# Nineteen of the 36 v tiles are issued from the POOL queue instead of SP

## The chip, the cores and the metric

One core of a Trainium2 chip runs the kernel. The metric is the device time of one launch in microseconds (us): the median of the runs. Work is spread over TensorE (PE in the profile), VectorE (DVE), ScalarE (ACT), GpSimd (POOL) and SyncE (SP), which only issues DMAs here. Each engine runs its own list of instructions in order, and they wait for each other through semaphores.

## The reference, cut to what matters

Attention within chunks of 64 rows, for 8 batches, 8 heads, 576 rows and 64 columns a head; then a channel mix on the rows of all heads (x, 4608 x 512).

```python
scores = scale * np.matmul(q_c, k_c.transpose(0, 1, 2, 4, 3))      # chunks of 64
attn = np.exp(scores - max); attn = attn / (sum(attn) + 1e-09)
out = np.matmul(attn, v_c)
# x = out with the heads side by side; x_prev = x one row earlier
xk = mu_k * x + (1.0 - mu_k) * x_prev
xr = mu_r * x + (1.0 - mu_r) * x_prev
k = np.maximum(xk @ w_k, 0.0)
v = k * k @ w_v
r = 1.0 / (1.0 + np.exp(-(xr @ w_r)))
return (r * v).astype(np.float32)
```

## The kernel before

The 4608 rows are cut into 36 tiles of 128 rows (t, two chunks each) and 18 groups of 256 rows (g, two tiles each). From group 4 on, two groups make a pair (p = 2 to 8), whose products with w_k and w_v are made by seven half-size products instead of eight, with sums of weights that are made once, stored to a DRAM tensor `kept` and fetched again for each pair from p = 3 on.

Nothing is scheduled by a planner: the work is cut into some 2,000 steps, and the string ORDER (lines 23 to 196) writes out the order by hand. A word such as `P12.1:A` is step 1 of task P12 on engine A (ScalarE; D is VectorE, G is GpSimd). The loop at the end of the function takes the words one by one, so each engine and each DMA queue gets its instructions in the order of the string. For a load, the letter is the queue: none or D means SP, A means ScalarE, G means GpSimd's queue, POOL (`queue`). Tiles lie at fixed columns of two SBUF arenas (`plain` and `rounded`; the table PLACE), and one stretch of columns serves many tiles in turn. An instruction that writes a stretch waits until the earlier reader of it is done; here a stretch that a tile waits for is called its slot.

The steps that the change and the prediction touch:

- `v{t}.0` (load_v, L491): loads the v tile of tile t, four DMAs of 64 KB, each 64 partitions x 4 heads x 64 elements of four bytes.
- `bq{g}`, `bk{g}` (load_blocks, L519 and L521): q and k of a group, in four steps each of 4 to 8 DMAs, from SP. VectorE turns them in blocks of 32 (att_qk, L689, `D{t}`).
- `S{t}` (L714): scores. `Z{g}`: softmax of a group on VectorE and ScalarE (L778 is its maximum, which waits for the scores of both tiles). `P{t}.0` (L831) transposes the weights, `P{t}.1` moves them, and `P{t}.2` (L844) multiplies them with the v tile into x; this is the only reader of v{t}.
- `K`, `R`, `V` of the first four groups (L1084, L1130, L1163), with `V{g}{tl}.8` (L1175) on VectorE, and for the pairs `M` (L1398), `C` (L1412), `F` (L1442), `V{n}_{p}` (L1488).
- `Y{n}{u}.2` (L1282) and `kr` (L1299): stores of weight sums to `kept`, from SP. `Xt4_3.1` (L1366) writes where the sum of Y41 lay, so it waits for that store.
- `L{n}{u}_{p}` and `Lr{i}_{p}` (L1305): fetches from `kept`, four or eight DMAs of 128 KB, from POOL. `Q{c}{tl}_{p}` (L1150): stores of the output of a pair, from POOL.

In ORDER v4 to v12 stand ahead of the first fetch and the first store of POOL. v17 stands between Q10_2 and L61_3, v20 between L61_4 and L40_4, v21 between Q00_3 and L60_4, v23 between L71_4 and L41_4, v24 between L61_5 and L50_5, v26 between L40_5 and L70_5, v30 between Q11_5 and Q01_5, v29 between L50_6 and Lr1_7, v32 between Q10_6 and L50_7, v35 between L51_7 and Lr0_8.

```python
def queue(e):
    return {"A": nc.scalar, "G": nc.gpsimd}.get(e, nc.sync)
...
        def fn(on):
            vt = new(f"v{t}", [HP, 2, D])
            ...
                    queue(on).dma_start(
```

Of the kernel before, what the change touches and what calls it, by code (L numbers as in the profile page):

```python
# [57 lines left out]
K30.0 V21.6 V21.7 bq6.1 bq7.3 kr.1 bq7.1 Ar4.0:D Z5.0:D Z5.1:D bq6.2 bq6.0 bq6.3 bk6.1 bk6.3 bk6.0
Z5.2:A Ar4.1:A Ak4.2:A Ak4.0:D D14.0:D D15.0:D Hr13.0:D Hr03.0:D Hr13.1:D Hr03.1:D A4.0:A Ak4.1:A
Z5.3:D Z5.4:D K31.3:D V20.8:D Y0.0:D Br4.0:D D13.0:D Bk4.1:D K30.1:A K30.2:A K30.3:A K30.4:D K32.0  # L60
P10.0 V31.0 P11.0 V21.8:D Hk14.0:D V30.0 V30.1 V31.1 K32.1:A K32.2:A U71.0:A Hr04.0:D V21.9 V20.9
bk7.3 bk7.0 U70.0:D P11.1:A U70.1:D K31.4:D K33.1:A V30.2 V30.3 V31.2 K33.2:A K33.3:A P10.1:D
K32.3:D U71.1:D K32.4:D D12.0:D Ar4.2:A K33.4:D V30.4 v11.0 v10.0 D13.1:D D12.1:D Br4.1:D Bk4.0:D
# [6 lines left out]
Hr15.0:A Hr15.1:D C21.0:A C21.1:D Y1.2:D Y71.0:A bk8.1 bk8.0 bk8.2 bq8.1 Ec11_20.1:A Xt4_2.0:A Y50.2  # L70
bq8.0 bk8.3 Y1.4:D D15.1:D D14.1:D Y70.2 V31.9 bq8.3 Y60.1:D Xt3_2.1:D Y1.5:D D16.1:D M20.4 C20.2:A
F1_20.0:A F1_20.1:D M20.5 P12.0 P13.0 M21.5 C20.3:A Ec11_21.0:A Y51.0:A M21.4 C21.2:A M20.6 V30.9
kr.0 Y51.1:D Y71.1:D Y60.2 v13.0 v12.0 Y61.0:D Ec11_21.1:A C21.3:A C20.5:D Ec22_20.0:A Hr05.0:A
P12.1:A Xt4_2.1:D D17.1:D M21.2 C21.4:D Ak9.0:D Hr05.1:D M20.2 P13.1:A Ec22_20.1:A C20.4:D Y61.1:D
M21.6 Ec21_21.0:A C21.5:D F4_20.0:A F4_20.1:D F1_21.0:D Ec21_21.1:A Ec22_21.0:A Ec21_20.0:A S14.0
# [11 lines left out]
D20.1:D Br7.0:D Bk7.0:D Z8.0:D X_3.0:D X_3.1:D X_3.2:D R61.0 M30.1 C30.0:A Hr07.0:A R60.1:A
Xt1_3.0:A Xt2_3.0:A Xb22_3.0:A R61.1:A M31.0 Xt1_3.1:D C30.1:D M31.1 Xt3_3.0:A C31.0:A Z8.1:D
X_3.3:D Xt2_3.1:D Q01_2.0 Y40.2 Q11_2.0 Q10_2.0 v17.0 L61_3.0 M30.4 bq10.0 bq9.0 bq9.3 bk9.2 Y51.2
L51_3.0 bk9.3 bk9.1 bk9.0 Y41.2 bq9.1 bq10.3 bq10.1 C31.1:D M30.5 M31.5 M31.4 A7.0:A Z8.2:A  # L90
Ec11_30.0:A Xt3_3.1:D Xb22_3.1:D Ec11_30.1:A C30.2:A D21.1:D Ec11_31.0:A C31.3:A Z8.3:D Z8.4:D M31.6
Xt4_3.0:D F1_30.0:A F1_30.1:D Xt4_3.1:D C30.3:A C31.2:A Hr17.0:A M30.6 C31.5:D Hr17.1:D C30.5:D
# [6 lines left out]
V5_3.0 F6_31.0:A F7_30.0:A R70.1:A O3.0:A v19.0 L71_3.0 L60_3.0 L70_3.0 Lr0_4.0 L40_3.0 L41_3.0
F_30.2:D F6_30.0:D F2_30.1:D Br8.0:D F6_30.1:D Br8.1:D P18.0 P19.0 V5_3.1 bq11.0 bq10.2 bq11.2  # L100
Ak8.1:A F2_31.0:A F6_31.1:D Ak8.0:D F7_31.1:D Bk8.0:D V2_3.0 Hr08.0:A Hk08.0:A V6_3.0 V6_3.1 O3.2:A
F2_31.1:D F7_30.1:D Hr18.0:D P18.1:D O3.1:A Ak8.2:A F_30.3:D D20.0:D V2_3.1 D21.0:D F_31.3:D P19.1:D
F3_31.0:A V7_3.0 V7_3.1 O3.3:D Hr08.1:D F3_30.0:D Hk08.1:D O3.6:D O3.4:D P18.2 P19.2 S20.0 S21.0
F3_31.1:D Z10.0:D Ar9.2:A Br9.1:D F3_30.1:D O3.8:D Lr1_4.0 M40.0 V4_3.0 V4_3.1 V3_3.0 Z10.1:D V3_3.1
Hr18.1:D Ak9.1:A Bk9.0:D Bk8.1:D R81.0 bq11.3 bq11.1 bk11.0 bk11.2 bk11.3 bk11.1 bq12.1 bq12.0
C40.0:A Ak9.2:A O3.5:D O3.9:D Hk18.0:A A9.0:A Ar9.1:A R81.1:A Bk9.1:D R80.0 R80.1:A Xb22_4.0:A
Hk18.1:D X_4.0:D O3.7:D X_4.1:D D22.0:D Xt1_4.0:D Xt1_4.1:D X_4.2:D M40.1 M41.0 Xt2_4.0:A Xt2_4.1:D
C40.1:D Br9.0:D M40.4 Ec11_40.0:D Xb22_4.1:D X_4.3:D M41.4 Xt3_4.0:D Hr09.0:D Z10.2:A C40.2:A
C41.0:A Ec11_40.1:A M40.5 M40.2 M41.5 C40.3:A C41.2:A M41.2 Xt3_4.1:D Z10.3:D Z10.4:D P20.0 M40.6
Xt4_4.0:A Hr19.0:A P21.0 Hr09.1:D D23.0:D C40.4:D bk12.2 bq12.3 L61_4.0 v20.0 C41.3:A M41.6 D23.1:D  # L110
Ec21_40.0:A Ec21_40.1:A C40.5:D D22.1:D Ec22_40.0:A Ec22_40.1:A P21.1:A F1_40.0:A C41.4:D P20.1:D
C41.5:D M41.1 C41.1:D Xt4_4.1:D L40_4.0 v22.0 bk13.3 Q10_3.0 L50_4.0 Q11_3.0 L70_4.0 Q01_3.0 Q00_3.0
v21.0 bq12.2 bq13.2 bk12.0 bk12.1 bk12.3 bq13.1 L60_4.0 L51_4.0 L71_4.0 v23.0 bq13.3 bk13.1 bk13.0
bk13.2 bq13.0 F1_40.1:D Ec22_41.0:A Ec22_41.1:A P20.2 S22.0 S23.0 P21.2 F4_40.0:A Z11.0:D F4_40.1:D
F4_41.0:A Ec11_41.0:A Ak10.1:A A10.0:A V1_4.0 M40.3 Ec21_41.0:A F_40.0:D Ec11_41.1:A F5_40.0:A
# [1503 lines left out]
```

## Time and profile before

| | us |
|---|---|
| median of 3 runs | 651.52 |
| lowest and highest | 649.33 and 654.31 |
| the profiled execution | 645.9 |
| its span, first to last instruction | 644.1 |
| busy in the span: TensorE, VectorE, ScalarE, POOL | 576.5, 530.0, 406.9, 181.2 |

The profile is of one execution. Busy time is that of an engine's own instructions; the issue of DMAs on SP isn't counted as busy, and "SPq" is SP's queue. A row of the timeline has the start, the length, the engine and line, the operation, its tiles as written <- read, and in brackets the idle time ahead of it with what ended it. A wait is put down to what came last.

### The profile page before, as it was taken

The numbers are of one execution on the slowest core, as the hardware profiler recorded it, in microseconds if no ns is written. First come the engines' busy times: TensorE is split into PE (matmuls) and PEld (weight loads), VectorE is DVE, ScalarE is ACT, GpSimd is POOL, SyncE is SP. The second block draws the span as 40 slices with busy tenths as digits, with TensorE's granted clock in tenths as the row PEclk, the third lists the DMA queues.
The fourth block names the chain that finished last, engine by engine and source line by source line (L and its number), as shares of the span: only waits on it lengthen the run. The fifth ranks groups of instructions, "written<-read, shape, count | busy, mean of one in ns | idle before, by whom it ended". The sixth has DMA issues, their size and how long they took to land.

```text
span 644.1 us, 16103 instructions
## 1 busy us (share of the span) xinstructions
PE 576.5 (90%) x6183; PEld 533.7 (83%) x6183; DVE 530.0 (82%) x889; ACT 406.9 (63%) x804; POOL 181.2 (28%) x338
## 2 busy tenths in 40 slices
...
GB/s 203 256 211 254 84 69 42 95 92 111 75 73 69 207 123 190 112 191 162 204 206 259 82 205 47 245 77 90 216 159 222 155 127 196 100 194 37 156 140 66
DMA packets 229438, 93.38 MB, mean 145 GB/s; under 512 B 181481, under 2 KB 221425, under 8 KB 229361
## 3 DMA queue, kind: packets, MB, share of 16 engines
...
## 4 chain that ended last, share of the span: by engine, by line
PE 53%; SPq 19%; DVE 12%; DMA 8%; issue 4%; ACT 4%; POOLq 0%; DVEq 0%; ACTq 0%; POOL 0%
PE o L1488 17%; PE m L1398 14%; SPq L521 14%; PE pr L1130 10%; SPq L491 4%; PE pv L1163 3%; DMA plain<-in_k 2%; PE xps L844 2%; PE s L714 2%; DMA plain<-in_v 2%; DMA plain<-in_q 1%; PE pt L831 1%; DVE plain L689 1%; ACT rounded L412 1%; DMA plain<-in_moe_w_v 1%
## 5 line engine op out<-in xcount | busy, mean ns | idle before, releaser
L1305 POOL DMA_DIRECT2D rounded<-kept x288 | 155.1, 555 | 372.4 <-PE pr L1130 256.6
L1398 PE MATMUL m<-rounded 128*128 128x256 f32 x1176 | 148.8, 286 | 12.4 <-DVE plain L1412 12.4
L1398 PEld LDWEIGHTS m<-rounded 128*128 128x128 f32 x1176 | 145.7, 194 | 14.1 <-DVE plain L1412 12.8
L1488 PE MATMUL o<-rounded 128*128 128x256 f32 x1176 | 151.2, 288 | 4.3 <-DVE rounded L1442 4.3
L1488 PEld LDWEIGHTS o<-rounded 128*128 128x128 f32 x1176 | 146.8, 195 | 6.0 <-DVE rounded L1442 4.7
L412 ACT ACTIVATE rounded<-plain 128x512 fp32r<-128x512 f32 (+1 forms) x151 | 97.3, 662 | 62.8 <-PE o L1488 13.6
L1130 PE MATMUL pr<-rounded 128*128 128x512 f32 x432 | 103.8, 394 | 0.1
L1130 PEld LDWEIGHTS pr<-rounded 128*128 128x128 f32 x432 | 80.2, 190 | 16.7 <-DVE plain L1506 0.5
L1007 ACT ACTIVATE plain<-xps,mu 128x256 f32<-128x256 f32 x128 | 54.3, 486 | 37.0 <-PE xps L844 21.7
L1442 DVE TENSOR_TENSOR rounded<-plain,rounded 128x512 fp32r<-128x512 f32 x98 | 65.6, 682 | 4.7 <-ACT rounded L412 2.0
L1013 ACT ACTIVATE plain<-xps,mu 128x255 f32<-128x255 f32 (+3 forms) x176 | 62.3, 448 | 0.0
L1084 PE MATMUL pk<-rounded 128*128 128x256 f32 x384 | 50.1, 290 | 9.8 <-DVE plain L1175 6.2
L1084 PEld LDWEIGHTS pk<-rounded 128*128 128x128 f32 x384 | 48.5, 197 | 12.2 <-issue 6.6
L689 DVE STREAM_TRANSPOSE plain<-plain 128x512 f32<-128x512 f32 x60 | 41.2, 698 | 19.1 <-DMA plain<-in_q 12.4
L844 PE MATMUL xps<-plain 64*64 64x64 f32 x1152 | 30.5, 241 | 24.9 <-DMA plain<-in_v 24.3
L844 PEld LDWEIGHTS xps<-plain 64*64 64x64 f32 x1152 | 25.3, 152 | 29.4 <-DMA plain<-in_v 19.5
L1163 PE MATMUL pv<-rounded 128*128 128x512 f32 x192 | 49.4, 409 | 0.0
L1024 DVE TENSOR_TENSOR plain<-plain 128x512 f32<-128x512 f32 x64 | 43.1, 680 | 2.0 <-ACT plain L1013 1.9
L1163 PEld LDWEIGHTS pv<-rounded 128*128 128x128 f32 x192 | 36.6, 197 | 7.5
L1073 ACT ACTIVATE plain<-plain 128x512 f32<-128x512 f32 x61 | 37.4, 628 | 5.0 <-DVE plain L1065 4.5
L778 DVE TENSOR_REDUCE mg<-s 128x16 f32<-128x1024 f32 x15 | 18.3, 1220 | 26.6 <-PE s L714 26.5
L1450 DVE TENSOR_TENSOR plain<-plain 128x512 f32<-128x512 f32 x56 | 38.0, 685 | 0.6
...
## 6 DMA issues: line engine op xcount, KB each, us to landing
rounded<-kept POOLq DMA_DIRECT2D x288, 128.0 KB, 3.6
plain<-in_v SPq DMA_DIRECT2D x144, 64.0 KB, 2.9
...
plain<-in_q SPq DMA_DIRECT2D x160, 32.0 KB, 2.3
plain<-in_k SPq DMA_DIRECT2D x160, 32.0 KB, 2.4
...
```

The lines of the kernel that those rows point to most:

```text
L412: nc.scalar.activation(to, x, AF.Copy)
L521: queue(e).dma_start(out=to_s[:, i], in_=of[:, i])
L844: nc.tensor.matmul(T[f"xps{g}"][halves[c], 2 * j + a, tl * TT + e * CH : tl * TT + (e + 1) * CH], T[f"v{t}"][halves[j], hp, e, :], T[f"pT{ ...
L1007: nc.scalar.activation(now(nm, h)[:, c], xps()[:, cb], AF.Copy, scale=mu2[:, 0, i, cb : cb + 1])
L1013: nc.scalar.activation(before(nm)[:, cb, s : s + n], xps()[:, cb, s - 1 : s - 1 + n], AF.Copy, scale=mu2[:, 1, i, cb : cb + 1],)
L1084: nc.tensor.matmul(pk[:, e, :], wk_at(f // 4)[:, a, cb, f % 4 * P : (f % 4 + 1) * P], x[:, b, cb, :], start=(n == 0), stop=(n == 3 * NB - 1),)
L1130: nc.tensor.matmul(pr, xr_at(g, a, cb)[:, tl * TT : (tl + 1) * TT], wr_of(g, cb // 2)[:, b, cb % 2, :], start=(n == 0), stop=(n == 3 * NB ...
L1163: nc.tensor.matmul(pv, kk_at(g, a, f // 2)[:, f % 2, tl * TT : (tl + 1) * TT], wv_at(f // 4)[:, :, b, f % 4, :], start=(f == 0 and n == 0) ...
L1305: nc.gpsimd.dma_start(out=to[:, c : c + 256], in_=of[:, c : c + 256])
L1398: nc.tensor.matmul(ps[w][:, e, :], left(n, a, cb, 2 * u + e), right(g, n, b, cb), start=first and i == 0, stop=i == 11, skip_group_check=True,
L1442: engine[e].tensor_tensor(form(p, n, u, 1), r(i), f32(form(p, n, u, 0)), ALU.subtract)
L1488: nc.tensor.matmul(ps[w][:, tl, :], form(p, n, u, a)[:, e, tl * TT : (tl + 1) * TT], moving(n, b, 2 * u + e), start=first and i == 0, stop ...
```

## The change

Nineteen words of ORDER get the ending `:G`, so the four DMAs of each of these tiles are issued on POOL's queue instead of SP's: v4, v5, v6, v7, v9, v8, v11, v10, v12, v17, v20, v21, v23, v24, v26, v30, v29, v32 and v35, in this order. Their place among the words stays, and so does everything else. The other seventeen (v0 to v3, v13 to v16, v18, v19, v22, v25, v27, v28, v31, v33, v34) stay on SP. The lines of the string are wrapped anew, which makes up most of the diff; three of its places:

```diff
-V01.1 V10.0 P4.0 V00.1 P5.0 K11.1:A cwv1.3:D hwv1.0:D hwv1.1:D K11.2:A P4.1:A V01.2 V00.2 v4.0 v5.0
-D6.0:D D7.0:D cwv2.3:D K13.3:A P5.1:A hwv2.0:A D7.1:D V00.3 S6.0 P4.2 S7.0 P5.2 V11.0 K13.4:D
+V01.1 V10.0 P4.0 V00.1 P5.0 K11.1:A cwv1.3:D hwv1.0:D hwv1.1:D K11.2:A P4.1:A V01.2 V00.2 v4.0:G
+v5.0:G D6.0:D D7.0:D cwv2.3:D K13.3:A P5.1:A hwv2.0:A D7.1:D V00.3 S6.0 P4.2 S7.0 P5.2 V11.0 K13.4:D
...
-Q10_5.0 Q11_5.0 bk17.3 bq17.3 Xt1_6.1:D Br13.0:D Xt2_6.1:D O5.7:D v30.0 R120.0 Q01_5.0 L60_6.0
+Q10_5.0 Q11_5.0 bk17.3 bq17.3 Xt1_6.1:D Br13.0:D Xt2_6.1:D O5.7:D v30.0:G R120.0 Q01_5.0 L60_6.0
...
-Hr116.0:A O7.3:D v34.0 v35.0 V3_7.1 O7.5:D Br16.0:D Hk016.1:D Hr016.0:D P34.2 P35.2 Hr116.1:D
+Hr116.0:A O7.3:D v34.0 v35.0:G V3_7.1 O7.5:D Br16.0:D Hk016.1:D Hr016.0:D P34.2 P35.2 Hr116.1:D
```

## Rows read from the trace of the kernel before

**Rows 1.** The page: busy time of TensorE; chain that ended last, by engine
```profile
PE 576.5 (90%) x6183; PEld 533.7 (83%) x6183; DVE 530.0 (82%) x889; ACT 406.9 (63%) x804; POOL 181.2 (28%) x338
...
PE 53%; SPq 19%; DVE 12%; DMA 8%; issue 4%; ACT 4%; POOLq 0%; DVEq 0%; ACTq 0%; POOL 0%
```

**Rows 2.** Waits: who waited for what, us in total, times, longest
```profile
DVE mg L778 <- PE s L714: 26.5, 5, 10.7
PE xps L844 <- DMA plain<-in_v: 24.3, 10, 8.2
...
DVE rounded L1366 <- DMA kept<-rounded: 13.6, 1, 13.6
...
DVE plain L689 <- DMA plain<-in_q: 12.4, 5, 6.6
...
DVE plain L689 <- DMA plain<-in_k: 6.6, 5, 3.6
```

**Rows 3.** Timeline of TensorE: the first matmuls behind its longest stops
```profile
87.81 0.47 PE L844 MATMUL xps<-plain 64*64 64x64 f32 x2 [4.34 <-DMA plain<-in_v]
...
163.99 1.41 PE L1084 MATMUL pk<-rounded 128*128 128x256 f32 x5 [6.23 <-DVE plain L1175]
...
183.63 1.02 PE L844 MATMUL xps<-plain 64*64 64x64 f32 x8 [8.00 <-DMA plain<-in_v]
...
292.28 6.66 PE L1398 MATMUL m<-rounded 128*128 128x256 f32 x36 [12.05 <-DVE plain L1412]
...
394.03 2.29 PE L1488 MATMUL o<-rounded 128*128 128x256 f32 x9 [3.62 <-DVE rounded L1442]
...
435.17 0.47 PE L844 MATMUL xps<-plain 64*64 64x64 f32 x2 [8.19 <-DMA plain<-in_v]
...
497.23 0.32 PE L844 MATMUL xps<-plain 64*64 64x64 f32 x2 [2.17 <-DMA plain<-in_v]
```

**Rows 4.** Busy time by stretch, PEclk the granted clock; one of seven, their sum
```profile
184.00:191.00 7.00, 6.59 (x132) 5.64 (x132) 1.78 (x3) 3.74 (x11) 0.00 (x0) 0.50 0.38 67
...
sum 37.00, PE 34.52 PEld 31.00 DVE 20.02 ACT 11.72 POOL 0.00; mean PE 4.93 PEld 4.43 DVE 2.86 ACT 1.67 POOL 0.00
```

**Rows 5.** Lines L491 and L1305: issues in ns (min/median/max); L1305's landing
```profile
L491 SPq DMA_DIRECT2D plain<-in_v x144: 595/614/1415, 3.6 to 547.3; - x144
...
L1305 POOL DMA_DIRECT2D rounded<-kept x288: 527/541/767, 237.1 to 619.0; - x144
...
DMA to landing us min/median/max: 2.5/3.6/5.8
```

**Rows 6.** Timeline of the SP queue: issues of v tiles, and of stores to kept
```profile
85.54 11.31 SPq L491 DMA_DIRECT2D plain<-in_v  x16
...
178.49 5.21 SPq L491 DMA_DIRECT2D plain<-in_v  x8
...
252.25 0.34 SPq L1282 DMA_DIRECT2D kept<-rounded  x1
266.91 2.58 SPq L491 DMA_DIRECT2D plain<-in_v  x4
...
284.86 0.45 SPq L1282 DMA_DIRECT2D kept<-rounded  x1
```

**Rows 7.** Timeline of VectorE: last readers of the slots of v4, v10, bq10; Xt4_3.1
```profile
65.76 1.22 DVE L603 TENSOR_TENSOR rounded<-plain,rounded 128x1024 fp32r<-128x1024 f32 x1
...
158.73 1.28 DVE L1045 TENSOR_TENSOR rounded<-plain,rounded 128x512 fp32r<-128x512 f32 x2
...
253.72 0.69 DVE L1442 TENSOR_TENSOR rounded<-plain,rounded 128x512 fp32r<-128x512 f32 x1 [0.29 <-PE o L1488]
...
289.73 0.69 DVE L1366 TENSOR_TENSOR rounded<-plain,rounded 128x512 fp32r<-128x512 f32 x1 [13.56 <-DMA kept<-rounded]
```

**Rows 8.** Timeline of POOL: its first DMAs, and the fetches around v24's place
```profile
237.15 6.15 POOL L1305 DMA_DIRECT2D rounded<-kept  x11 [219.37 <-PE pr L1130]
...
410.24 1.60 POOL L1305 DMA_DIRECT2D rounded<-kept  x3 [0.67 <-issue]
```

More of the change, by code (lines that the diff above doesn't have):

```diff
@@ L58 @@
[L58 to L63, printed above, removed]
@@ L70 @@
[L70 to L75, printed above, removed]
@@ L87 @@
[L87 to L92, printed above, removed]
@@ L99 @@
[L99 to L104, printed above, removed]
@@ L105 @@
[L105 to L115, printed above, removed]
-Ec21_41.1:A Ec12_40.0:A Hr19.1:D Z11.1:D F_40.1:D Ak10.0:D Bk10.0:D F_40.2:D D24.0:D Ar10.0:D
@@ L129 @@
-Q11_4.0 L51_5.0 Q10_4.0 L61_5.0 v24.0 L50_5.0 M51.4 M50.1 Xb22_5.0:A C50.1:D Z12.2:A Z12.3:D M51.5
-C51.3:A Ar11.2:A Xb22_5.1:D Ec11_50.0:D Z12.4:D Br11.1:D M50.4 C50.2:A M50.5 C50.3:A C51.2:A M51.6
-Xt4_5.0:A C51.5:D Xt4_5.1:D Ec11_50.1:D P24.0 P25.0 M50.6 M51.2 M50.2 C50.5:D F1_50.0:D D29.0:D
-C51.4:D M51.1 Ec21_51.0:D Hr011.0:A C50.4:D Hr011.1:D Ec22_50.0:A Ec22_50.1:A F4_50.0:A F4_50.1:D
-F1_50.1:D Ak12.0:D Hr111.0:A Ec22_51.0:A Ec21_51.1:A Ec22_51.1:A F4_51.0:A Ec21_50.0:D Ec21_50.1:A
-P24.1:A C51.1:D M50.3 M51.3 V1_5.0 Ec11_51.0:D F4_51.1:D Ec11_51.1:A P25.1:A S26.0 P24.2 P25.2 S27.0
+Ar2.1:A A2.0:A v6.0:G v7.0:G Ak2.2:A Br2.0:D Ak2.0:D Bk2.1:D D8.1:D Bk2.0:D Hk02.0:D Ar2.2:A
@@ new lines @@
+Hr02.0:A V01.8:D Hk02.1:D V00.8:D Br2.1:D Hk12.0:D Hk12.1:D K22.0 U1.1:D U0.4:D bq4.1 bq4.2 bq4.3
+bq4.0 U1.4:D D8.0:D V10.8:D Hr12.0:A U50.0:D P7.1:A P6.1:A S8.0 P6.2 P7.2 Ak3.0:D U50.1:D D9.0:D
+V11.8:D Hr02.1:D Hr12.1:D S9.0 U0.2:D U0.3:D bq5.2 V01.9 bq5.0 bk5.2 bq5.3 bq5.1 V11.9 bk5.0 V00.9
+bk5.3 V10.9 bk6.2 Ak3.2:A Bk3.1:D U1.6:D U0.5:D U1.3:D U1.5:D Hk13.0:A Hk13.1:D Z4.0:D K20.0 K20.1:A
+K21.0 R21.0 R20.0 U51.0:A Ak3.1:A K20.2:A Z4.1:D Bk3.0:D U0.6:D U1.7:D Z4.2:A K21.1:A Hk03.0:D
+K20.3:D Hk03.1:D D11.0:D U60.0:D K22.1:A U31.0:A Ar3.2:A Z4.3:D U60.1:D A3.0:A R20.1:A U61.0:A
@@ new lines @@
+K20.4:D U0.7:D Ar3.0:D Z4.4:D K22.2:A K21.2:A K21.3:A K21.4:D U51.1:D K31.0 U30.0:D R21.1:A Br3.1:D
+D10.0:D U30.1:D U61.1:D K22.3:A K23.0 V21.0 V21.1 V20.0 V20.1 V20.2 P8.0 K31.1:A K22.4:D K23.1:A
+K31.2:A Ar3.1:A Br3.0:D U31.1:D P9.0 P9.1:A K23.2:A v9.0:G v8.0:G P8.1:D bq7.2 bk5.1 bq7.0 D11.1:D
+D10.1:D V21.2 V20.3 V20.4 K23.3:A K23.4:D Ar9.0:D V20.5 V21.3 P8.2 P9.2 S10.0 S11.0 V21.4 V20.6
+K33.0 V20.7 V21.5 K30.0 V21.6 V21.7 bq6.1 bq7.3 kr.1 bq7.1 Ar4.0:D Z5.0:D Z5.1:D bq6.2 bq6.0 bq6.3
+bk6.1 bk6.3 bk6.0 Z5.2:A Ar4.1:A Ak4.2:A Ak4.0:D D14.0:D D15.0:D Hr13.0:D Hr03.0:D Hr13.1:D Hr03.1:D
@@ new lines @@
+A4.0:A Ak4.1:A Z5.3:D Z5.4:D K31.3:D V20.8:D Y0.0:D Br4.0:D D13.0:D Bk4.1:D K30.1:A K30.2:A K30.3:A
+K30.4:D K32.0 P10.0 V31.0 P11.0 V21.8:D Hk14.0:D V30.0 V30.1 V31.1 K32.1:A K32.2:A U71.0:A Hr04.0:D
+V21.9 V20.9 bk7.3 bk7.0 U70.0:D P11.1:A U70.1:D K31.4:D K33.1:A V30.2 V30.3 V31.2 K33.2:A K33.3:A
+P10.1:D K32.3:D U71.1:D K32.4:D D12.0:D Ar4.2:A K33.4:D V30.4 v11.0:G v10.0:G D13.1:D D12.1:D
+Br4.1:D Bk4.0:D V30.5 P10.2 P11.2 S12.0 S13.0 Hk14.1:D Hk04.0:D Hk04.1:D Z6.0:D Ak5.0:D V31.3
+Hr04.1:D Ak5.1:A Y0.3:D Y1.1:D Hr14.0:D V31.4 V31.5 R31.0 V30.6 V31.6 V30.7 V31.7 R30.0 Ar5.1:A
@@ new lines @@
+Ak5.2:A Bk5.0:D Y0.1:D Y0.2:D R31.1:A Y70.0:A Y0.4:D Y50.0:A Ar5.0:D Hr14.1:D Z6.1:D Y0.5:D Bk5.1:D
+Z6.2:A V31.8:D X_2.0:D X_2.1:D Y70.1:D Xb22_2.0:A Xb22_2.1:D Z6.3:D R40.0 M20.0 Xt3_2.0:A R30.1:A
+Y50.1:D Br5.0:D X_2.2:D Z6.4:D R40.1:A Ar5.2:A A5.0:A C20.0:A M20.1 C20.1:D Ec11_20.0:A Y60.0:A
+V30.8:D Y1.3:D Br5.1:D Y1.0:D R41.0 Xt2_2.0:A Xt1_2.0:A R41.1:A X_2.3:D M21.0 M21.1 Xt1_2.1:D bk7.1
+bk7.2 Xt2_2.1:D Hr15.0:A Hr15.1:D C21.0:A C21.1:D Y1.2:D Y71.0:A bk8.1 bk8.0 bk8.2 bq8.1 Ec11_20.1:A
@@ new lines @@
+Xt4_2.0:A Y50.2 bq8.0 bk8.3 Y1.4:D D15.1:D D14.1:D Y70.2 V31.9 bq8.3 Y60.1:D Xt3_2.1:D Y1.5:D
+D16.1:D M20.4 C20.2:A F1_20.0:A F1_20.1:D M20.5 P12.0 P13.0 M21.5 C20.3:A Ec11_21.0:A Y51.0:A M21.4
+C21.2:A M20.6 V30.9 kr.0 Y51.1:D Y71.1:D Y60.2 v13.0 v12.0:G Y61.0:D Ec11_21.1:A C21.3:A C20.5:D
+Ec22_20.0:A Hr05.0:A P12.1:A Xt4_2.1:D D17.1:D M21.2 C21.4:D Ak9.0:D Hr05.1:D M20.2 P13.1:A
+Ec22_20.1:A C20.4:D Y61.1:D M21.6 Ec21_21.0:A C21.5:D F4_20.0:A F4_20.1:D F1_21.0:D Ec21_21.1:A
+Ec22_21.0:A Ec21_20.0:A S14.0 P12.2 S15.0 P13.2 F1_21.1:D Y1.6:D Y1.7:D Ec21_20.1:A Z7.0:D
@@ new lines @@
+Ec22_21.1:A F4_21.0:D Ak6.0:D F_20.0:D A6.0:A Ak6.1:A Bk6.0:D Z7.1:D F_20.1:D F_20.2:D Ar6.1:A
+Ar6.0:D V1_2.0 M21.3 M20.3 F4_21.1:D Ec12_20.0:A F_21.0:D F5_20.0:A F5_20.1:D F_21.1:D V1_2.1 R50.0
+Z7.2:A F6_20.0:A R51.0 F_21.2:D Z7.3:D bk10.3 v14.0 Y71.2 bq8.2 bk10.2 bk10.1 R50.1:A Ec12_20.1:A
+O2.0:A V5_2.0 F2_20.0:A F6_21.0:D F6_20.1:D Z7.4:D Ec12_21.0:A R51.1:A V6_2.0 F5_21.0:A Ec12_21.1:A
+F7_20.0:A F6_21.1:D D17.0:D F2_20.1:D D16.0:D P14.0 V6_2.1 F7_20.1:D Br6.0:D F2_21.0:A Hk06.0:A
+O2.2:A F7_21.0:A P15.0 F2_21.1:D V2_2.0 F_20.3:D F7_21.1:D V7_2.0 F3_20.0:D F_21.3:D Hk06.1:D
@@ new lines @@
+F5_21.1:D P14.1:A Ak6.2:A Ar6.2:A P15.1:A V2_2.1 F3_20.1:D Y0.6:D Bk6.1:D V7_2.1 Y41.0:D Y0.7:D
+V5_2.1 Y40.0:A O2.3:D Y40.1:D Br6.1:D bk10.0 Y61.2 v15.0 bq9.2 S16.0 S17.0 P14.2 P15.2 O2.1:A V3_2.0
+Y41.1:D F3_21.0:A Hr16.0:A F3_21.1:D Ar7.0:D O2.4:D O2.6:D Ak7.2:A Lr0_3.0 Lr1_3.0 M30.0 V3_2.1
+Hr06.0:A Ar7.2:A Ak7.1:A Hk16.0:A Ak7.0:D O2.8:D Bk7.1:D O2.5:D Hr06.1:D V4_2.0 Ar7.1:A Hr16.1:D
+V4_2.1 R60.0 O2.7:D Br7.1:D Hk16.1:D O2.9:D D20.1:D Br7.0:D Bk7.0:D Z8.0:D X_3.0:D X_3.1:D X_3.2:D
+R61.0 M30.1 C30.0:A Hr07.0:A R60.1:A Xt1_3.0:A Xt2_3.0:A Xb22_3.0:A R61.1:A M31.0 Xt1_3.1:D C30.1:D
@@ new lines @@
+M31.1 Xt3_3.0:A C31.0:A Z8.1:D X_3.3:D Xt2_3.1:D Q01_2.0 Y40.2 Q11_2.0 Q10_2.0 v17.0:G L61_3.0 M30.4
+bq10.0 bq9.0 bq9.3 bk9.2 Y51.2 L51_3.0 bk9.3 bk9.1 bk9.0 Y41.2 bq9.1 bq10.3 bq10.1 C31.1:D M30.5
+M31.5 M31.4 A7.0:A Z8.2:A Ec11_30.0:A Xt3_3.1:D Xb22_3.1:D Ec11_30.1:A C30.2:A D21.1:D Ec11_31.0:A
+C31.3:A Z8.3:D Z8.4:D M31.6 Xt4_3.0:D F1_30.0:A F1_30.1:D Xt4_3.1:D C30.3:A C31.2:A Hr17.0:A M30.6
+C31.5:D Hr17.1:D C30.5:D Ec22_31.0:A Ec11_31.1:D Ec22_31.1:A Ec22_30.0:A Ec22_30.1:A D19.1:D M31.2
@@ new lines @@
+C31.4:D D18.1:D F1_31.0:A F1_31.1:D D18.0:D v16.0 P16.0 P17.0 M30.3 M31.3 D19.0:D F4_31.0:A
+F4_31.1:D Ec21_31.0:D P17.1:A P16.1:A M30.2 S18.0 Ec21_31.1:A Ec12_31.0:A F4_30.0:D Hr07.1:D S19.0
+C30.4:D Z9.0:D P16.2 P17.2 Ec21_30.0:A F_31.0:D F5_31.0:A Ec21_30.1:A F4_30.1:D Z9.1:D Z9.2:A
+F_30.0:D F_31.1:D F_31.2:D F5_30.0:D F_30.1:D F5_30.1:D R71.0 R70.0 V1_3.0 L50_3.0 v18.0 Ec12_30.0:A
+Ar8.2:A Ec12_30.1:A F2_30.0:A Z9.3:D Ar8.0:D F5_31.1:D Z9.4:D Ec12_31.1:A R71.1:A Q00_2.0 Ar8.1:A
+F7_31.0:A V1_3.1 V5_3.0 F6_31.0:A F7_30.0:A R70.1:A O3.0:A v19.0 L71_3.0 L60_3.0 L70_3.0 Lr0_4.0
```

92 lines of the change are left out of this document (41 added, 51 removed).

## The prediction

> **What bounds the kernel now.** I read the page's first part and the chain first. TensorE is busy 576.5 us of 644.1, so 68 us at most are idle on the engine that carries the work. The chain that ended last gives TensorE 53%, but 19% to the issue on the SP queue and 8% to DMAs [rows 1]: a queue that only hands out loads holds about 122 us of it. The reader should ask next whether TensorE really stands still for those loads. The waits say yes: it waited 24.3 us for v tiles, in ten pieces [rows 2]. VectorE waited 12.4 and 6.6 us for q and k loads, 13.6 us for the landing of a store to `kept`, and 26.5 us for scores that come behind a late tile; together 59.1 us [rows 2].
>
> The timeline of TensorE then gives each stop a place. I number the seven that matter by what ended them [rows 3]: (a) 4.34 us before 87.81, v4; (b) 6.23 before 163.99, VectorE at L1175; (c) 8.00 before 183.63, v10; (d) 12.05 before 292.28, VectorE at L1412; (e) 3.62 before 394.03, VectorE at L1442; (f) 8.19 before 435.17, v24; (g) 2.17 before 497.23, v28. Their sum is 44.60 us. Each stop also costs clock: in seven stretches behind them, 37 us together, the granted clock is at or near 0.50, the lower of its two levels, as in the one shown, and TensorE is busy 34.52 us there [rows 4]; the same work at the higher level needs about half, so up to 17.3 us lie there.
>
> **Why the loads are late.** SP takes 614 ns to issue one v DMA [rows 5], four to a tile, 2.6 us with the gaps (four tiles in 11.31 us [rows 6]). Nineteen tiles are 19 x 2.6 = 49 us of a queue that issues one instruction after the other. Tile v10 is handed out from 181 to 184, in the second half of the eight issues from 178.49 [rows 6], while its slot had been free since the subtraction that ends by 160.0 [rows 7]; v4 goes out at 85.54 although the last reader of its slot ended at 67.0 [rows 6, 7]. So these tiles are late because of SP's place in its list, not because of memory.
>
> **The change part by part.** Nothing is removed; 76 DMAs go to another queue.
>
> *SP loses 49 us of issue.* (a), (c) and (f) are waits for tiles that move. v4 to v12 are nine tiles, and POOL is empty where they stand: it idles 219.37 us before its first DMA at 237.15, so since 17.8 [rows 8]. So v4 and v10 go out when their slots come free, at 67.0 and 160.0, 18 and 21 us before they did. v24 stands on POOL behind the fetch that ends near 411, 16 us ahead of the stop at 427.0 [rows 8, 3]; its slot holds k10, read last by the scores of tiles 20 and 21, far earlier. (g) waits for v28, which stays on SP but stands behind v30 and v29 in the order; both leave, two tiles are 5.2 us [rows 6], and the stop is 2.17. These four: 22.70 us.
>
> (b) comes from a VectorE wait of up to 6.6 us for a q load [rows 2]. Six tiles have left SP ahead of it: four of 11.31 us and two more of about 5.2, 16.5 us [rows 6]. (a) takes 4.3 of that lead, because TensorE and VectorE come earlier too, so 12 us stay against 6.6 and the 2 us of the k wait before it. The cover is thin, and a slot that comes free late could use it up.
>
> (d) is the largest. SP stops after the store at 252.25 and starts again with v17 at 266.91: 14.3 us in which the whole queue stood behind v17's slot [rows 6]. Eight blocks later it issues the store of a `kept` block at 284.86 [rows 6], and VectorE's wait of 13.56 us ends at 289.73, just behind that landing [rows 7]; L1412 follows, and TensorE goes on at 292.28. With v17 on POOL, SP goes on once bq10's slot is free, at 254.4 [rows 7]; the work from the end of v17 at 269.5 to that store was 15.3 us, so it is issued at 269.7 and, with the same 4.8 us to land, is there at 274.5. VectorE came to it at 276.2. (d) goes, by 1.7 us. Behind v17 on POOL wait the fetches of pair 3, which it holds until about 271 (266.9 and 4.4); they are in rival 2.
>
> (e) comes from VectorE, which waits for k and q loads just before: the longest of its k waits, 3.6 us [rows 2]. v20, v21 and v23 leave SP ahead of them: 3 x 2.6 = 7.8 us. It goes.
>
> *POOL gains 76 issues.* No v DMA was on POOL, so the price is bounded: a fetch there takes 541 ns for 128 rows of 1 KB [rows 5], and a v DMA has 256 rows of 256 B. Flat, it is 0.55 us; if it goes with the rows, 1.1. I take the upper end, as the rows are what differ: 4.4 us a tile. For the first nine tiles that hides in POOL's idle time [rows 8]. The other ten put 22 to 44 us more between the weight fetches; these are issued ahead of their use, and what it costs if that cover is gone is rival 2. A v DMA lands about as late as a fetch, 3.6 us [rows 5], against the 16 us that v24 has.
>
> *A rule that speaks against the change.* The 288 fetches were issued in 527 to 767 ns each, over 380 us of the run, and landed in 5.8 us at the latest [rows 5]. The Trainium skill, "SBUF — State Buffer", section "SBUF: two separate sides", says that DMAs from the POOL queue have their descriptors written by GpSimd, which VectorE locks out during some copies. By that rule an issue beside such a copy would be stretched, by the row it is stretched to 767 ns at most, 3.1 us a tile; the sum is the same by the row, and the rule's case is the third rival below.
>
> **The sum.** 44.60 us idle in full. Of the 17.3 us at the lower clock I take half, 8.6: not each stop will close wholly, and VectorE's own waits, 59.1 us, cap what both engines can gain. Total 53 us. Against the execution's own time, 645.9 us (span 644.1 and 1.8 around it), that is 593. The median of the runs shown is 651.5, 5.6 above that execution; I carry the 53 over: 598.5, and call it 599.
>
> **The rivals.**
>
> 1. *Only the direct waits go.* SP's freed time is eaten: it stops in order at the next slot that is not free, as it does at v17, and q, k and the store come no earlier. Then (a), (c), (f), (g) remain, 22.70 of 44.60 us, with their share of the clock 27: 624.5 us. For it: SP already stands still at one place [rows 6], so issue is not its only limit. Against it: at (d) the tile on which it stands is one of those that leave.
>
> 2. *The fetches pay.* Ten of the tiles stand among the weight fetches on POOL, 2.2 to 4.4 us each. If all of that delayed weights that TensorE waits for, 22 to 44 us come back: 620 to 642, say 631. Against it: none of its seven stops is for a fetch, the largest waits of TensorE are for v tiles and VectorE [rows 2, 3].
>
> 3. *Slower: POOL is held at each issue.* The eight tiles v4 to v10 go out one behind the other from 67.0, 32 DMAs. At X us each v10 is there at 67.0 + 32 X; TensorE wants it at 175.6 and got it at 183.6. With each DMA held as long as the slowest landing, 5.8 us, that is 252.6, 69 us later than now, and what (d) to (g) still give, about 31, does not pay for it: 690. It decides from X = (183.6 - 67.0 + 31) / 32 = 4.6 us on. The Trainium skill's rule of the section above would be its cause. Against it: 767 ns is the longest of 288 [rows 5].
>
> 4. *No change.* The tiles would still be late, say because they wait for their slots and not for SP. Against it: 18 and 21 us between free slot and issue. 651.5.
>
> **How the numbers follow.** The forecast has 0.70; rival 1 0.17, rival 2 0.07, rival 3 0.03, rival 4 0.03. The prediction is the likeliest, 599. Low end: all 44.6 and all 17.3 us, and some 4.6 from smaller stops not counted: 585. High end: rival 1, 624. That leaves out rivals 2 in part, 3 and 4, and ends below 585: under 2 in 10. About 1% is what a measurement of this kernel can tell from no change (its three runs spread by 0.8%). Faster by over 1%: 0.70 + 0.17 + 0.07 = 0.94; same 0.03; slower 0.03.
>
> **What would show it.** Right: TensorE's wait for in_v falls from 24.3 to under 5 us; VectorE's wait for `kept` is gone; SP's 14.3 us hole is filled with q and k issues; the low-clock stretches behind the stops are gone; L491 on POOL takes 0.55 to 1.1 us an issue. Wrong: L491 on POOL over 2 us; new waits of L1488 or L1130 for L1305's fetches (rival 2); VectorE still waiting for q and k at (b) and (e) (rival 1). The forecast is wrong above all if closing these stops brings another engine's limit forward at once: VectorE works through most of the time between them, and then the clock's part and some of (b), (d), (e) don't come.

## The result: 587 us, 9.8% faster

| | before | after |
|---|---|---|
| median (us) | 650.42 (648.69 to 654.31, 4 runs) | 586.96 (586.52 to 587.40, 4 runs) |
| ratio | | 0.9017, 95% interval 0.8973 to 0.9061 |
| profiled execution, its span (us) | 645.9, 644.1 | 586.77, 584.9 |
| TensorE busy, idle in the span (us) | 576.5, 67.6 | 563.1, 21.8 |
| POOL busy (us) | 181.2 | 229.3 |

The profiled execution lost 59.1 us: 45.8 of TensorE's idle time (67.6 less 21.8) and 13.4 of its busy time (576.5 less 563.1). The matmuls are the same 6183, and the second part is clock: summed over stretches of 2 us of each trace, TensorE's busy time times (1 less its granted clock) is 19.4 us before and 6.0 after, 13.4 less, and the rest of its busy time is 557.1 and 557.2. All line numbers of after from L492 on are one higher than before. From the page of after, busy times and the granted clock in 40 slices:

```profile
PE 563.1 (96%) x6183; PEld 522.9 (89%) x6183; DVE 527.4 (90%) x889; ACT 406.6 (70%) x804; POOL 229.3 (39%) x414
...
PEclk9889999999999999999999999999999999999999
```

Beside [rows 1], TensorE went from 90% to 96% of its span. The clock row is below 9 only near the start.

The waits of TensorE and of VectorE in after (us in total, times, longest) answer to [rows 2]:

```profile
PE pk L1085 <- ACT plain L1143: 1.9, 1, 1.9
PE o L1489 <- DVE rounded L1443: 1.8, 1, 1.8
...
DVE plain L690 <- DMA plain<-in_k: 4.6, 4, 2.4
...
DVE plain L690 <- DMA plain<-in_q: 0.7, 1, 0.7
```

No row of TensorE names in_v any more (24.3 us before), none of VectorE names `kept` (13.6), and its q wait fell from 12.4 to 0.7. From the timeline of TensorE, the only matmuls after 60 us with more than 1 us idle before them:

```profile
127.85 4.62 PE L1085 MATMUL pk<-rounded 128*128 128x256 f32 x24 [1.93 <-ACT plain L1143]
...
165.15 1.05 PE L715 MATMUL s<-plain 64*64 64x64 f32 x36 [1.13 <-issue]
...
352.24 4.34 PE L1489 MATMUL o<-rounded 128*128 128x256 f32 x34 [1.78 <-DVE rounded L1443]
```

Of the seven stops of [rows 3], (a), (b), (c), (d), (f) and (g) are gone, and 1.78 us of (e) are left, the third row. Of (b) nothing stayed in this execution; its matmuls follow without a wait:

```profile
152.49 3.11 PE L1085 MATMUL pk<-rounded 128*128 128x256 f32 x24
```

The first row is a stop that was there before too (2.86 us) and was not counted among the seven. The second is new: these scores stand behind the place of (c), and VectorE's transposition (L690) ahead of them, which had waited 1.32 us for a k load, ends at 165.04.

Three timelines of after show where the tiles went. POOL, the issues of v4, v10, v17 and of v24's first piece:

```profile
70.33 2.06 POOL L492 DMA_DIRECT2D plain<-in_v  x3 [53.03 <-PE pr L1131]
...
148.57 1.85 POOL L492 DMA_DIRECT2D plain<-in_v  x3 [11.18 <-DVE rounded L1046]
...
245.28 1.87 POOL L492 DMA_DIRECT2D plain<-in_v  x3 [4.29 <-DVE rounded L1367]
...
369.16 0.71 POOL L492 DMA_DIRECT2D plain<-in_v  x1 [0.28 <-issue]
```

SP, at the place of the hole of [rows 6]:

```profile
230.21 0.34 SPq L1283 DMA_DIRECT2D kept<-rounded  x1
232.39 3.96 SPq L522 DMA_DIRECT2D plain<-in_q  x8
...
248.47 0.45 SPq L1283 DMA_DIRECT2D kept<-rounded  x1
```

VectorE, the subtraction of [rows 7] that had waited 13.56 us:

```profile
254.15 0.69 DVE L1367 TENSOR_TENSOR rounded<-plain,rounded 128x512 fp32r<-128x512 f32 x1
```

v4 goes out at 70 instead of 85.5, v10 at 148.6 instead of 181. Behind the store at 230.21 SP stands for 1.8 us instead of 14.3, the next store leaves at 248.47, and VectorE doesn't wait.

POOL's price for a v DMA, from line L492's issues (ns, min/median/max):

```profile
L492 POOL DMA_DIRECT2D plain<-in_v x76: 615/624/810, 70.3 to 500.7; - x76
```

and from the page's DMA issues (KB each, median us to landing):

```profile
plain<-in_v POOLq DMA_DIRECT2D x76, 64.0 KB, 2.5
```

### The profile page after: what moved, and what is told of

It reads as the page before. It is cut to its first block, busy times and chain, and to the rows that moved or that the text cites. A ratio compares the mean times of both kernels' runs of the same rounds, so it can differ in the third digit from the quotient of the medians.

```text
span 584.9 us, 16200 instructions
## 1 busy us (share of the span) xinstructions
PE 563.1 (96%) x6183; PEld 522.9 (89%) x6183; DVE 527.4 (90%) x889; ACT 406.6 (70%) x804; POOL 229.3 (39%) x414
## 5 line engine op out<-in xcount | busy, mean ns | idle before, releaser
L1489 PE MATMUL o<-rounded 128*128 128x256 f32 x1176 | 147.9, 284 | 2.1 <-DVE rounded L1443 1.8
L1399 PE MATMUL m<-rounded 128*128 128x256 f32 x1176 | 147.0, 284 | 0.6 <-DVE plain L1503 0.4
L1489 PEld LDWEIGHTS o<-rounded 128*128 128x128 f32 x1176 | 143.7, 192 | 3.5 <-DVE rounded L1443 2.0
L1399 PEld LDWEIGHTS m<-rounded 128*128 128x128 f32 x1176 | 143.5, 192 | 2.7 <-PE o L1489 0.8
L492 POOL DMA_DIRECT2D plain<-in_v x76 | 47.8, 631 | 194.1 <-PE pr L1131 53.0
L1164 PE MATMUL pv<-rounded 128*128 128x512 f32 x192 | 47.2, 396 | 0.0
L690 DVE STREAM_TRANSPOSE plain<-plain 128x512 f32<-128x512 f32 x60 | 41.3, 700 | 5.6 <-DMA plain<-in_k 4.6
L1151 POOL DMA_DIRECT2D out<-plain x28 | 15.7, 561 | 73.1 <-DVE plain L1507 46.9
L1164 PEld LDWEIGHTS pv<-rounded 128*128 128x128 f32 x192 | 35.0, 188 | 7.0
L415 DVE CAST rounded<-plain 128x512 fp32r<-128x512 f32 (+1 forms) x76 | 32.0, 432 | 3.3 <-PE m L1399 2.1
```

The costliest lines, as they stand in the source:

```text
L492: queue(on).dma_start(out=vt[j * CH : (j + 1) * CH, :, e, :], in_=v[b, j * HP : (j + 1) * HP, c * CH : (c + 1) * CH, :].rearrange("h t d - ...
L1164: nc.tensor.matmul(pv, kk_at(g, a, f // 2)[:, f % 2, tl * TT : (tl + 1) * TT], wv_at(f // 4)[:, :, b, f % 4, :], start=(f == 0 and n == 0) ...
L1399: nc.tensor.matmul(ps[w][:, e, :], left(n, a, cb, 2 * u + e), right(g, n, b, cb), start=first and i == 0, stop=i == 11, skip_group_check=True,
L1489: nc.tensor.matmul(ps[w][:, tl, :], form(p, n, u, a)[:, e, tl * TT : (tl + 1) * TT], moving(n, b, 2 * u + e), start=first and i == 0, stop ...
```

## The experiments

All times are medians beside runs of the kernel before on the same chip; the theory is the one of the prediction. Not all of them ran on one chip, so the ratios serve to compare one changed kernel with another.

**Three parts of the change, each alone.** Only words of the order change; the first of each part is shown.

```
e1_early  -v4.0  +v4.0:G      and v5 to v12
e2_v17    -v17.0 +v17.0:G
e3_late   -v20.0 +v20.0:G     and v21 v23 v24 v26 v30 v29 v32 v35
```

> Only the nine tiles v4 to v12 are issued on POOL. Theory (each stop of TensorE has its own late load): stops (a), (b) and (c) go, 18.6 us idle; the whole change saved 59 us for 46 us less idle, 1.29 us of time per us of idle, so 24 us: ratio 0.963, and TensorE's 12 us stop before its M matmuls stays, ended by VectorE after the kept store. Rival (what counts is how much issue SP is rid of, 59 us over 19 tiles, 3.1 us a tile): 9 tiles give 28 us, ratio 0.957. Rival (tiles were late for their slots): no change.

> v17 alone is issued on POOL. Theory: SP's hole of 14.3 us is the hold of one tile's slot, so one tile gives the whole of stop (d), 12.05 us and its clock, 15.5 us: ratio 0.976; TensorE's waits for v tiles stay at 24 us. Rival (issue time of SP counts): one tile of 19 gives 3 us, ratio 0.995.

> The nine tiles behind v17 are on POOL, v4 to v12 and v17 stay on SP. Theory: stops (e), (f), (g) go, 14 us idle, 18 us with the clock: ratio 0.972; the stop (d) of 12 us stays. Rival (SP's issue time counts): 28 us, ratio 0.957. Rival (the fetches on POOL pay): under 10 us, ratio over 0.985.

Measured: e1_early 624.07 us, ratio 0.9615 (0.9561 to 0.9669); e2_v17 635.14, 0.9787 (0.9727 to 0.9848); e3_late 625.22, 0.9630 (0.9561 to 0.9699). Their product is 0.906, the full change 0.9017: the parts add up. One tile, v17, is worth 2.1%, as the theory says and the price per tile does not. For e1_early the two expectations lie too close to be told apart. From the timeline of TensorE in e1_early, the row of (d) and that of (f):

```profile
270.06 6.43 PE L1398 MATMUL m<-rounded 128*128 128x256 f32 x36 [12.04 <-DVE plain L1412]
...
414.71 0.47 PE L844 MATMUL xps<-plain 64*64 64x64 f32 x2 [9.94 <-DMA plain<-in_v]
```

So SP's lead from nine tiles does nothing for (d): SP arrives earlier and stands behind v17's slot all the same (14.3 us again in its timeline). e3_late gave some 6 us more than expected. Its page:

```profile
PE 569.8 (92%) x6183; PEld 528.7 (85%) x6183; DVE 528.1 (85%) x889; ACT 406.4 (65%) x804; POOL 205.1 (33%) x374
```

With a span of 620.7 us the idle time is 50.9, 16.7 less than before where 14 were expected, and the busy time is 6.7 less where 4 were: half of the miss is idle time that was not counted, and half is the clock behind the closed stops, which was rated too low as in the prediction.

**Order or queue.** Everything stays on SP, and v17's word moves behind bq10.1:

```
-Q10_2.0 v17.0 L61_3.0 M30.4 bq10.0 ... bq10.3 bq10.1 C31.1:D
+Q10_2.0 L61_3.0 M30.4 bq10.0 ... bq10.3 bq10.1 v17.0 C31.1:D
```

> No tile on POOL: v17 stays on SP, but its word stands 23 steps later, behind bq10.1. Theory (SP is held in order behind a slot that is not free): the same as with v17 on POOL, less its own 2.6 us of issue: 13 to 15 us, ratio 0.977 to 0.980. Rival (the second queue itself is what helps): no change, ratio 1.00.

Measured: 638.39 us, 0.9821 (0.9754 to 0.9888), against 0.9787 with v17 on POOL; the intervals overlap. (The word moved 15 places, not 23.) In both kernels VectorE no longer waits for `kept`, and the 36 matmuls of L1398 that (d) held back have no wait ahead of them; the first row is of e2_v17, the second of e4_v17_later:

```profile
280.80 4.55 PE L1398 MATMUL m<-rounded 128*128 128x256 f32 x36
...
282.36 4.55 PE L1398 MATMUL m<-rounded 128*128 128x256 f32 x36
```

Stop (d) is a matter of what stands behind a word that must wait for its slot. No second queue is needed for it.

**The direct waits alone.** v4, v5, v11, v10 and v24 go to POOL, in the same way.

> Only v4, v5, v10, v11 and v24 are on POOL, the tiles for which TensorE stood still. Theory: (a), (c), (f) go and SP is rid of 13 us, which covers part of (b): 20.5 us idle and up to 6: 26 to 34 us with the clock, ratio 0.948 to 0.960; (d) stays. Rival (SP's issue time counts, 3.1 us a tile): 16 us, ratio 0.976.

Measured: 623.23 us, 0.9631 (0.9586 to 0.9676), nearer to the theory. From the timeline of TensorE:

```profile
130.22 4.63 PE L1084 MATMUL pk<-rounded 128*128 128x256 f32 x24 [4.28 <-ACT plain L1142]
...
160.52 4.93 PE L1084 MATMUL pk<-rounded 128*128 128x256 f32 x24 [5.80 <-DVE plain L1175]
...
278.74 6.92 PE L1398 MATMUL m<-rounded 128*128 128x256 f32 x36 [12.74 <-DVE plain L1412]
```

(a), (c) and (f) are gone, and (d) is whole. (b) keeps 5.80 us: of the five tiles only v4 and v5 stand ahead of it on SP, and of their 5.2 us the closed stop (a) takes 4.3.

**Is it SP's issue time or the bytes?** The changed kernel, with an additional copy to a spare buffer on SP at each place that a v DMA left. The result does not use the copies. e5_dummy copies the same 64 KB in 256 rows, e10_load the same bytes in 4 rows, e12_tiny one row of 256 bytes:

```
+if on == "G":
+    nc.sync.dma_start(out=spare[t, e, j], in_=v[b, j*HP:(j+1)*HP, c*CH:(c+1)*CH, :].rearrange("h t d -> t h d"))
 e10_load: ... .rearrange("h t d -> h (t d)")
 e12_tiny: in_=v[b, j*HP, c*CH, :]
```

> The changed kernel, and at each old place of the 19 tiles SP issues four DMAs of the same rows from v to a spare DRAM tensor that nothing reads: the tiles come early, but SP has its 49 us of issue again (the extra copies are left out of the result). Theory: the stops that end with a tile on POOL, (a), (c), (f), stay away, and (d), whose cause is the hold at v17's slot; (b), (e), (g), which end with SP's other loads, come back wholly or in part: up to 12 us idle, 0 to 15 us slower than the changed kernel, 587 to 602, ratio to before 0.902 to 0.926. Rival (only the v tiles themselves were late): 587, ratio 0.902. Rival (SP's issue time is the whole cause): back to 640 or more.

> The changed kernel with 76 additional copies on SP at the places of the moved loads, as the run with 256 rows of 256 bytes had them and with the same bytes, but each as 4 rows of 16 KB. The result does not use the copies. Theory (SP's issue time is what brought 28 us back there, 76 times about 0.61 us): if an issue of 4 rows takes under 0.1 us, the time stays at 587 to 593 us, and SP's lead is as in the changed kernel. Rival (the bytes on the DMA engines brought it back): 605 to 615 us although SP issues faster. If an issue of 4 rows takes as long as one of 256, the time is that of the other run, 610 to 618 us, and the two stay apart only by SP's row.

> The changed kernel with 76 additional copies on SP at the places of the moved loads, each of one row of 256 bytes (19 KB in all, against 4.98 MB of the copies of 64 KB). The result does not use the copies. An issue of 256 rows took SP 0.61 us and one of 4 rows 0.56 us, so one row should take it 0.55 us and SP gets back 42 of the 47 us of issue time that the change took from it, and nearly no bytes. Theory (it is the issue time that brought 28 us back): 610 to 617 us, and VectorE and ScalarE wait again for bk6, V00.9 and bk13 at the places of the run with 64 KB. Rival (it is the bytes): 586 to 592 us, although SP is as busy issuing.

Measured: 614.58 us, 0.9498 (0.9450 to 0.9546); 615.56, 0.9466 (0.9419 to 0.9512); 616.18, 0.9465 (0.9382 to 0.9547). SP's issues of the copies in ns (min/median/max), one fence for each kernel in this order:

```profile
L493 SPq DMA_DIRECT2D spare<-in_v x76: 547/610/1556, 86.2 to 506.5; - x76
```

```profile
L493 SPq DMA_DIRECT2D spare<-in_v x76: 558/559/749, 86.5 to 506.6; - x76
```

```profile
L493 SPq DMA_DIRECT2D spare<-in_v x76: 495/587/2019, 87.2 to 507.0; - x76
```

e5_dummy came out between its two expectations, and e10_load could not tell the two apart, because 4 rows cost SP nearly as much as 256. e12_tiny settles it: with 0.02 MB instead of 4.98 MB the same 28 to 29 us come back. It is the issue time. Where they come back, from the timeline of TensorE in e12_tiny (L720 answers to L714 of before, L1090 to L1084, L1494 to L1488):

```profile
113.86 1.14 PE L720 MATMUL s<-plain 64*64 64x64 f32 x32 [6.64 <-DVE plain L695]
...
135.78 5.49 PE L1090 MATMUL pk<-rounded 128*128 128x256 f32 x24 [4.01 <-ACT plain L1148]
...
165.78 5.46 PE L1090 MATMUL pk<-rounded 128*128 128x256 f32 x24 [4.34 <-DVE plain L1181]
...
373.26 5.82 PE L1494 MATMUL o<-rounded 128*128 128x256 f32 x34 [6.50 <-DVE rounded L1448]
```

These are (b), (e) and two more behind late q, k and stores. (a), (c), (d) and (f), the waits for v tiles and for v17's slot, do not return; of (g), which waits for v28 on SP, 1.31 us do. So with SP as busy as before the change still gives 5%, as e8_direct (3.7%) and e2_v17 (2.1%) do together, and SP's freed time is the other half.

**POOL's price.** Each v DMA on POOL is cut in four, one per head, 16 issues to a tile:

```
+step = 1 if on == "G" else HP
+for h in range(0, HP, step):
     queue(on).dma_start(out=vt[..., h : h + step, e, :], in_=v[b, j*HP+h : j*HP+h+step, ...])
```

> The changed kernel with each v DMA on POOL cut into four, one head each: 16 issues a tile instead of 4. Theory: POOL has room, the early tiles wait for nothing and the late ones are ahead of their use by several us: at some 0.55 us an issue a tile takes 8.8 us instead of 2.5, and the time rises by 0 to 8 us, 587 to 595, ratio 0.902 to 0.915. Rival 2 of the prediction (the fetches pay for what stands among them): ten tiles x 6.3 us, up to 63 us slower, 650.

Measured: 601.99 us, 0.9304 (0.9258 to 0.9350), 15 us slower than the change by the medians and 19 by the ratios: beyond the theory, far from the rival. Issues on POOL, from line L493:

```profile
L493 POOL DMA_DIRECT2D plain<-in_v x304: 516/536/1106, 69.0 to 521.3; - x152
```

and the wait of TensorE that came back:

```profile
PE xps L846 <- DMA plain<-in_v: 12.0, 9, 2.1
```

64 rows cost POOL 536 ns, 256 rows 624: nearly a price per DMA. The page gives all 304 issues 159.1 us of POOL, against 47.8 for the 76: 111 us more on POOL cost 15 us of time.

**More on POOL.** e7_all sends all tiles from v4 on to POOL; e9_hold adds only v27 to the change.

```
e7_all   v13 v14 v15 v16 v18 v19 v22 v25 v27 v28 v31 v33 v34: +:G
e9_hold  -v27.0 +v27.0:G
```

> All tiles from v4 on are issued on POOL, 13 more than in the change. Theory: SP's v tiles are hardly waited for any more (TensorE idles 22 us in all, 15 of them in the first 40 us or for ScalarE), only the wait for bk13.2 is left to gain: 0 to 3 us faster than the changed kernel, ratio 0.897 to 0.902. Rival (SP's issue time still counts): 13 x 3.1 = 40 us, 547. Rival (POOL is full, tiles whose slots come free late hold the fetches): slower than the changed kernel, over 590.

> The changed kernel with one more tile, v27, issued from the POOL queue at its place in the order. Theory (a v tile whose place comes before its slot is free holds what stands behind it in its queue): with all tiles on POOL, v27 held POOL for 11.3 us (326.3 to 337.6) and the fetches Lr0_5 and Lr1_5 behind it came late: TensorE waited 6.8 us for them at 352 to 362. Here the same stop, 5 to 8 us, and at 1.29 us of time per us of stop 6 to 10 us: 593 to 597 us. Rival (the 26 us that all tiles on POOL lost come from the issue time of 52 more DMAs, 33 us): one tile more is 2.5 us of issue, 584 to 589 us, and no wait for a fetch of kept at TensorE.

Measured: e7_all 613.24 us, 0.9490 (0.9427 to 0.9552); e9_hold 588.11, 0.9065 (0.9030 to 0.9099). From e7_all, POOL's timeline and then TensorE's:

```profile
337.62 1.84 POOL L491 DMA_DIRECT2D plain<-in_v  x3 [11.32 <-DVE rounded L414]
...
354.67 2.48 PE L1130 MATMUL pr<-rounded 128*128 128x512 f32 x5 [2.17 <-DMA rounded<-kept]
...
449.30 0.51 PE L844 MATMUL xps<-plain 64*64 64x64 f32 x8 [2.57 <-DMA plain<-in_v]
...
512.11 0.47 PE L844 MATMUL xps<-plain 64*64 64x64 f32 x2 [4.55 <-DMA plain<-in_v]
```

and the same places in e9_hold:

```profile
338.98 1.83 POOL L491 DMA_DIRECT2D plain<-in_v  x3 [11.78 <-DVE rounded L414]
...
355.88 1.89 PE L1130 MATMUL pr<-rounded 128*128 128x512 f32 x7 [1.15 <-DMA rounded<-kept]
...
359.34 0.93 PE L1130 MATMUL pr<-rounded 128*128 128x512 f32 x3 [1.57 <-DMA rounded<-kept]
```

v27 held POOL as long in both (11.3 and 11.8 us), but alone it left 2.7 us of stops (1.15 and 1.57) where I expected 5 to 8 and e7_all has 6.8. My reading of e7_all, that a word held by its slot explains its first loss, fell in its size: alone the hold is mostly absorbed, and the time is not told apart from the change's. e7_all loses more at that place, where v25 stands behind v27, and again at v28 and v33, which stand among fetches. How its 26 us divide between held words and POOL's longer list was not tried further.

**A version that goes on.** The change, with v19 on POOL too and V00.9 earlier on SP:

```
-v19.0  +v19.0:G
-bq5.3 bq5.1 V11.9 bk5.0 V00.9 bk5.3
+V00.9 bq5.3 bq5.1 V11.9 bk5.0 bk5.3
```

> The changed kernel with two further words: v19 on POOL, so that SP reaches bk13.2 some 2.6 us earlier (VectorE waited 3.0 us for it at 345.5 and TensorE 1.8 us at 350.5), and V00.9 ahead of bq5.3 on SP, so that it lands some 9 us earlier (ScalarE's K22.1 waited for it, and TensorE 1.9 us behind that at 125.9). Theory: both stops go, 3.7 us of TensorE's idle, at 1.29 us per us 4.8 us: 581 to 584 us. Rival (other work ends just behind those two waits, and gives the time back): 585 to 588 us.

Measured: 582.10 us (579.68 to 588.23, 6 runs), 0.8977 (0.8939 to 0.9014). The page:

```profile
PE 558.8 (96%) x6183; PEld 518.6 (89%) x6183; DVE 527.0 (91%) x889; ACT 406.7 (70%) x804; POOL 232.4 (40%) x418
```

and, from the timeline of TensorE, the only stop over 1 us that is left after 60 us, at the place of (b):

```profile
149.85 3.11 PE L1084 MATMUL pk<-rounded 128*128 128x256 f32 x24 [1.66 <-DVE plain L1175]
```

Both stops are gone, as the theory said. Its median is 5 us below the changed kernel's, but the intervals of the two ratios overlap, and they were not timed side by side: probably better, not shown.

## Why the prediction was right, and 12 us off

**The mechanism** was right. The tiles were late because of SP's place in its list, and the forecast's own signs came in: in_v from 24.3 us to none listed, `kept` from 13.6 to none, the 14.3 us hole to 1.8.

**The stops.** The forecast had 44.60 us of idle go in full; 45.8 went. The seven stops gave 42.8 (44.60 less the 1.78 left); smaller ones, which it had left out, gave the other 3.0, the new 1.13 us taken off. It called the cover of (b) thin: (b) closed in this execution, but in e1_early and e9_hold, with the same words up to that place, 1.94 and 2.26 us of it stayed. (The wait of 2 us before it, which the forecast put down to a k load, was for q.) It had (e) go, and 1.78 us stayed behind a late k load; e11_best, which takes v19 off SP too, has no such stop.

**Stop (d)** was worked out to the microsecond. VectorE's subtraction came at 276.2 before and at 254.15 after, 22.0 us earlier; the store at 248.47 is 270.5 on the old scale, and the forecast said 269.7. The margin behind its landing was forecast at 1.7 us, and no wait was left.

**The clock** is the term that was mis-sized: 8.6 us taken, 13.4 measured; the forecast's bound was 17.3 for seven stretches, and all of the trace of before has 19.4. The reason given, that not each stop would close wholly and VectorE's waits would cap the gain, did not hold: VectorE's busy share rose from 82% to 90%, and behind the first 60 us TensorE has only three stops over 1 us left. Each microsecond of idle time was worth 1.29 us of time (59.1 over 45.8).

**The scale.** The 53 us were worked out on a profiled execution of 645.9 us and carried over to a median of 651.5. The medians differ by 63.5, the two profiled executions by 59.1. After's runs lie within 0.9 us of each other, before's within 5.6, and before's spans go loosely with the clock (645.4 us at 0.951 and 650.9 at 0.941 in two of its runs, but 646.5 at 0.940 in a third); I take it that a longer execution of before has more of the stops and low clock that the change removes, which is argued and not shown. So the 12 us are 4.8 of clock, 1.2 of idle time, 4.4 of this scale, 1.1 because the median of before came out at 650.4, and rounding.

**POOL's price** was taken at the upper bound, 1.1 us; it is 0.624, near the flat one. It changed nothing here, as the sum had it hidden. e6_split4, with 159.1 / 19 = 8.4 us of issue a tile where the upper bound was 4.4, lost 15 us; so rival 2, with 22 to 44 us for ten such tiles, was priced too dear.

**The rivals.** Rival 1 was well sized: e8_direct, nearly its content, gives 24 us where it said 27. It did not come because v17 left SP, which e1_early, e2_v17 and e4_v17_later show, and because SP's freed issue time reaches the q and k loads, which e12_tiny shows. The Trainium skill, "Trainium Kernel Development and Optimization", section "Key Constraints", says that DMAs issued from several engines share the same DMA engines, and that only the issue time is saved. The runs here agree on the issue time: that saving is worth the 28 to 29 us which came back with 0.02 MB. They show a second gain beside it, the 34 us that e12_tiny keeps with SP as busy as before, from words that no longer stand behind a slot or behind other words. Rival 3 needed 4.6 us an issue; the longest of 76 was 810 ns. The Trainium skill's rule of VectorE locking out POOL's descriptor writing during some copies ("SBUF — State Buffer", section "SBUF: two separate sides") speaks for such a hold. With VectorE busy 90% of the span the trace shows none of that size; whether VectorE makes such copies here, no run shows.

## What to carry to other kernels

Look for the queue that the chain of waits names, and then for the one word in its list that waits for a slot: what stands behind it is late by the whole hold, and moving the word back cures it as well as another queue. SP's time was counted in DMAs here, not in bytes, so a second queue is worth its free time; but not without limit: with all tiles from v4 on there, 26 us of the gain were lost, and how they divide was not shown. A stop of TensorE can cost more than its length, as the granted clock can fall behind it: here each us of idle time that went was worth 1.29 us of time.

## What the runs showed of the chip

The issue of a DMA had nearly one price for all that was tried (medians in ns): on SP 559 ns for 4 rows of 16 KB, 587 for one row of 256 bytes and 610 for 256 rows of 256 bytes; on POOL 536 for 64 rows and 624 for 256. I had thought that 4 rows might take under 0.1 us. On POOL a v DMA landed 2.5 us after its issue (median), the 68 that stayed on SP after 4.4, where all 144 had a median of 2.9 before; those that stayed stand in other stretches, so the queues themselves are not compared by this. After a stop the granted clock fell in after too: it was 0.79 from 127 to 135 us, behind the stop of 1.93 us. But it does not fall behind each: around the stop of 1.78 us before 352.24 it stayed at 1.00, as it did before the change from 134 to 138 us, behind the stop of 2.86 us (the rows are busy time by stretch: its length, the busy time of PE, PEld, DVE, ACT and POOL, the granted clock, the DMA share, GB/s):

```profile
127.00:135.00 8.00, 7.15 (x36) 6.71 (x37) 5.39 (x10) 7.08 (x15) 0.78 (x2) 0.79 0.38 61
...
350.00:358.00 8.00, 5.99 (x43) 5.41 (x43) 7.22 (x13) 2.15 (x4) 0.00 (x0) 1.00 0.32 51
```
